# Two DMA transposes in place of PE transposes, and paired elementwise work, in the last job of a cross-network kernel

## The chip, the cores and the metric

The kernel runs on 1 core of one Trainium2 chip. The metric is the device time of one execution, in microseconds (us); smaller is better. PE is the TensorE matmul engine, PEld its weight load, ACT ScalarE, DVE VectorE, POOL GpSimd, and SP the engine whose queue issues most DMAs here ("SPq" in the profile; "ACTq" is ACT's queue). The profile's span is the time from the first to the last instruction on the core. It is about 1.8 us shorter than the measured time. A DMA is issued when a queue starts on it, and it has landed when all its bytes are there and those who wait for it may go on; from issue to landing it is called in flight.

## The reference

```python
B, F, D, L = 16384, 26, 16, 6          # Din = 26 * 16 = 416
x0: (16384, 416)   ws: (6, 416, 416)   bs: (6, 416)   # all bf16

def reference(x0, ws, bs):
    x = x0
    for l in range(6):
        proj = jnp.einsum('bd,de->be', x, ws[l]) + bs[l]
        x = x0 * proj + x
    return x
```

Each layer is a product with a 416 x 416 matrix, a bias, a multiplication by the input x0, and the addition of the residual x.

## The kernel before

The 16,384 rows are cut into 8 groups of 2,048 rows (0 to 7; `LAST` is 7), each of 4 chunks `j` of 512 rows. Features lie on the partitions: 416 is three tiles of 128 features (`NT = 3`) and a tail of 32. A job is one layer of one group; 48 jobs run in an order that lets the groups overlap. Except in the very last job, results are feature-major, so each finished group has to be turned to row-major by DMA transposes into the buffer `ost` before it can be stored:

```python
def output(g):
    s, s3 = xset[(g, L)], xtail[(g, L)]
    def turn(t):                                   # one feature tile, all 2,048 rows
        add("sp", lambda h: h.dma_start_transpose(
            ost[:, :, t * P:(t + 1) * P], xs[s][:, t * GC:(t + 1) * GC]),
            reads=[("x", s, t, j) for j in range(NJ)], writes=[("ost", t)], lane="ot", batch=g)
    turn(0)
    # ... the tail of 32 features: a DMA transpose into ot3 and a POOL copy into ost ...
    turn(1)
    turn(2)
    # ... one store of 2,048 x 416 values, 1.70 MB, from ost to out ...
```

`add` puts an instruction on an engine's queue and works out semaphore waits from the declared reads and writes. `turn(2)` of group 6 is called "the last output transpose" below, and the store after it "the store of group 6".

The last job (group 7, layer 5) is computed row-major, so that its result can be stored without a turn. It needs the residual row-major as well, and the kernel before turns it on PE (a product with the identity) for all three feature tiles, then copies it out of PSUM:

```python
def turn_main(kp, bks, ts):          # 128 x 128 PE transposes: 48 in all
    for j in range(NJ):
        for h2 in range(2):
            for t in ts:
                add("pe", ... h.transpose(psum_t(bks[j])[:, o:o + P], xcol(t, j, kk), ident[:, :]) ...)

def rows_out(kp, bks):               # PSUM -> x5n, 832 wide, 3 on ACT and 5 on DVE
    ...

def nat_mul(kk, j, b):               # evict on ACT, multiply by x0 on DVE, 416 wide
    add("act", lambda h: h.activation(o, bank(b, n=D), ACT_F.Copy), ...)
    add("dve", lambda h: h.tensor_tensor(o, o, x0v, ALU.mult), ...)
    # (the very last one multiplies straight out of PSUM, on DVE)

def nat_add(kk, j):                  # add the residual on DVE, 416 wide
    add("dve", lambda h: h.tensor_tensor(o, o, x5v, ALU.add), ...)

def nat_store(k0, k1, j0, j1, eng="sp"):
    dst = out[LAST * GC:B, :].rearrange("(j p k) f -> p j k f", j=NJ, k=KK)[:, j0:j1, k0:k1, :]
    add(eng, lambda h: h.dma_start(dst, on[:, j0:j1, k0:k1, :]), ...)
...
nat_store(0, 2, 0, NJ)               # after kk = 1: 832 KB, in runs of 2 rows = 1,664 bytes
...                                  # then 4 pieces after kk = 2 and during kk = 3, the last one from ACT's queue
```

In this order, (j p k), each partition holds 4 adjacent rows, and the four sub-blocks `kk` are strided columns of the chunk.

## Time and profile before

| kernel before | |
|---|---|
| median, 6 runs | 478.88 us (478.71 to 481.38) |
| span of the profiled run | 476.7 us |
| PE / DVE / ACT busy | 470.2 / 406.9 / 342.4 us |

From the page of the kernel before, the span, the busy times and the chain of waits (the dependences followed back from the last instruction, by engine):

```profile
span 476.7 us, 8467 instructions
...
PE 470.2 (99%) x3403; PEld 198.7 (42%) x3403; DVE 406.9 (85%) x714; ACT 342.4 (72%) x371; POOL 7.2 (2%) x14
...
PE 92%; SPq 4%; DVE 2%; ACT 1%; DMA 0%; issue 0%
```

PE bounds the kernel as a whole. The change touches only the end, so that end has to be read by itself. I call the first weight load of the last job its start. It is one line of the timeline of the kernel before (start in us, duration in us, then engine, line, operation, and destination <- source):

```profile
457.67 1.11 PEld L770 LDWEIGHTS ps<-ident,x 128*128 128x128 bf16 x16
```

The last pieces of the chain in the kernel before (start, duration, what; "..." stands for lines left out, some of them steps of 0.01 to 0.02 us called issue):

```profile
470.15 0.67 PE ps L800 x3
...
470.84 0.52 ACT x L828
...
471.37 0.53 ACT x L828
...
471.92 0.38 DVE x L830
...
473.56 0.51 DVE x L825
...
474.09 0.38 DVE x L835
```

At the end the chain goes from PE to ACT to DVE; the last addition ends at 474.47.

The DMA engines have their own story. Here are the last output transpose and the store of group 6 in SP's timeline of the kernel before (start, time to issue):

```profile
459.11 1.43 SPq L636 DMA_TRANSPOSE ost<-x  x1
464.19 0.38 SPq L655 DMA_DIRECT2D out_dram<-ost  x1
```

And this is what the DMA engines did afterwards, in stretches of the kernel before (the stretch and its length, the busy time of PE, PEld, DVE, ACT and POOL with their instruction counts, then PE's clock, the busy share of the 16 DMA engines, and GB/s; a share a little above 1 means overlapping packets):

```profile
465.50:468.50 3.00, 3.00 (x24) 1.57 (x22) 2.98 (x10) 2.51 (x6) 0.00 (x0) 1.00 1.05 351
468.50:470.00 1.50, 1.50 (x15) 0.65 (x13) 1.50 (x6) 1.47 (x4) 0.00 (x0) 1.00 1.10 335
470.00:472.50 2.50, 2.38 (x16) 1.28 (x12) 2.25 (x9) 1.77 (x4) 0.00 (x0) 1.00 1.06 376
473.00:474.00 1.00, 0.00 (x0) 0.00 (x0) 0.97 (x3) 0.00 (x0) 0.00 (x0) 1.00 0.24 83
474.00:475.50 1.50, 0.00 (x0) 0.00 (x0) 0.43 (x2) 0.00 (x0) 0.00 (x0) 1.00 0.92 321
```

The stores of groups 6 and 7 together are 3.41 MB, and they keep the DMA engines full from 465.2 to 473.0. Only then is there a hole, because the last pieces are not computed yet. So the kernel before is bound by compute at its end, with less than 1 us of spare DMA time.

### The profile page before, as it was taken

The page shows a single profiled execution, that of the slowest core. Times are in us where ns is not written, and L with a number is a line of the kernel's source. Part 1 is how long each engine was busy: PE and PEld are TensorE (multiplying, and loading weights), DVE is VectorE, ACT ScalarE, POOL GpSimd, SP SyncE. Part 2 cuts the span into 40 slices and gives each one's busy share as a digit, 9 for nine tenths or more (in the row PEclk, how much of TensorE's full clock was granted, in tenths as well). Part 3 has the DMA queues.
Part 4 walks back from the last instruction along what each step waited for, and adds up shares of the span by engine and source line. Part 5 has one row for each costly group of instructions (what it writes and reads, how often), then busy time and mean ns, then how long its engine had stood idle before and what let it go on. Part 6 is the DMA issues. An engine that isn't in the chain of part 4 may idle for free.

```text
span 476.7 us, 8467 instructions
## 1 busy us (share of the span) xinstructions
PE 470.2 (99%) x3403; PEld 198.7 (42%) x3403; DVE 406.9 (85%) x714; ACT 342.4 (72%) x371; POOL 7.2 (2%) x14
## 2 busy tenths in 40 slices
PE   8999999999999999999999999999999999999996
PEld 6344444444444444444444444434444444444353
DVE  2888888888888888898888879888888888888897
ACT  4677777777777777777777777777777777777775
POOL 0000000000000000000000000000000000000000
PEclk9999999999999999999999999999999999999999
DMA  8886920720102477379219932970000138026388
GB/s 232 179 176 144 195 66 1 157 65 1 34 1 46 76 212 156 75 168 242 57 35 211 207 80 40 189 236 0 2 15 21 26 64 231 0 45 159 108 145 286
DMA packets 131851, 52.27 MB, mean 110 GB/s; under 512 B 108122, under 2 KB 130404, under 8 KB 131812
## 3 DMA queue, kind: packets, MB, share of 16 engines
q1 hardware_dynamic: 131064, 51.20, 46.8%
q8 instruction: 26, 0.43, 0.4%
q10 hardware_dynamic: 748, 0.54, 0.3%
q14 instruction: 13, 0.11, 0.1%
HBM read 5.97 MB, written 13.63 MB: 41 GB/s over the span
## 4 chain that ended last, share of the span: by engine, by line
PE 92%; SPq 4%; DVE 2%; ACT 1%; DMA 0%; issue 0%
PE ps L456 75%; PE ps L477 7%; PE ps L497 7%; SPq L292 2%; PE ps L800 1%; PE ps L471 1%; DVE x L408 1%; DVE tw L403 1%; SPq L297 1%; PE ps L488 1%; SPq L285 0%; SPq L521 0%; ACT tw L394 0%; PE ps L770 0%; DMA x<-ost 0%; SPq L304 0%
## 5 line engine op out<-in xcount | busy, mean ns | idle before, releaser
L394 ACT ACTIVATE tw<-ps,bias 128x1024 bf16<-128x1024 f32 (+1 forms) x295 | 299.8, 1071 | 120.0 <-PE ps L477 75.9
L456 PE MATMUL ps<-x,wm 128*128 128x512 bf16 x1692 | 379.4, 379 | 0.0
L456 PEld LDWEIGHTS ps<-x,wm 128*128 128x128 bf16 x1692 | 159.0, 98 | 213.2 <-issue 28.3
L403 DVE TENSOR_TENSOR tw<-tw,x 128x1024 bf16<-128x1024 bf16 (+1 forms) x285 | 192.7, 685 | 53.9 <-ACT tw L394 53.6
L408 DVE TENSOR_TENSOR x<-tw,x 128x1024 bf16<-128x1024 bf16 (+1 forms) x285 | 182.5, 681 | 0.0
L477 PE MATMUL ps<-x,w 32*128 32x512 bf16 x512 | 39.2, 379 | 0.2 <-DMA x<-ost 0.2
L497 PE MATMUL ps<-x,wm 128*32 128x512 bf16 x564 | 33.0, 380 | 0.0
L434 ACT ACTIVATE ts<-ps,bias 128x512 bf16<-128x512 f32 x47 | 28.8, 701 | 0.0
L438 DVE TENSOR_TENSOR x<-ts,x 128x512 bf16<-128x512 bf16 x47 | 18.6, 417 | 3.0 <-DMA x<-x 3.0
L497 PEld LDWEIGHTS ps<-x,wm 128*32 128x32 bf16 x564 | 13.8, 96 | 17.6 <-issue 5.3
L477 PEld LDWEIGHTS ps<-x,w 32*128 32x128 bf16 x512 | 7.8, 92 | 27.9 <-issue 27.1
L436 DVE TENSOR_TENSOR ts<-ts,x 128x512 bf16<-128x512 bf16 x47 | 18.6, 418 | 0.0
L643 POOL COPY ost<-ot 128x512 bf16<-128x512 bf16 x7 | 6.3, 900 | 449.9 <-DMA ot<-x 449.9
L800 PE MATMUL ps<-wm,x 128*128 128x416 bf16 x48 | 9.4, 341 | 0.0
L568 DVE COPY x<-ps 128x512 bf16<-128x512 bf16 x4 | 1.7, 425 | 8.0 <-PE ps L561 8.0
L828 ACT ACTIVATE x<-ps 128x416 bf16<-128x416 f32 x15 | 7.1, 525 | 1.3 <-PE ps L800 1.1
L565 ACT ACTIVATE x<-ps 128x512 bf16<-128x512 bf16 x8 | 4.3, 594 | 4.8 <-PE ps L561 4.8
L800 PEld LDWEIGHTS ps<-wm,x 128*128 128x128 bf16 x48 | 5.1, 115 | 3.8 <-issue 1.4
L488 PE MATMUL ps<-x,w 32*32 32x512 bf16 x188 | 5.9, 374 | 0.0
L830 DVE TENSOR_TENSOR x<-x,x 128x416 bf16<-128x416 bf16 x15 | 5.4, 368 | 0.3 <-ACT x L828 0.2
L471 PE MATMUL ps<-x,w 32*32 32x512 bf16 x208 | 5.6, 385 | 0.0
L835 DVE TENSOR_TENSOR x<-x,x 128x416 bf16<-128x416 bf16 x16 | 5.6, 369 | 0.1
(35 smaller groups left out, 43.2 us busy)
## 6 DMA issues: line engine op xcount, KB each, us to landing
out_dram<-ost SPq DMA_DIRECT2D x7, 1664.0 KB, 6.8
x<-in_x_dram SPq DMA_DIRECT2D x7, 416.0 KB, 7.1
x<-x SPq DMA_DIRECT2D x24, 96.0 KB, 2.2
wm<-in_ws_dram SPq DMA_DIRECT2D x5, 312.0 KB, 3.4
x<-x SPq DMA_DIRECT2D x22, 64.0 KB, 2.0
x<-ost SPq DMA_DIRECT2D x28, 32.0 KB, 2.3
out_dram<-x SPq DMA_DIRECT2D x1, 832.0 KB, 4.3
x<-x SPq DMA_DIRECT2D x24, 32.0 KB, 1.9
```

The lines of the kernel that those rows point to most:

```text
L394: add("act", lambda h, a=a, w=w, b0=b0: h.activation(tw[r][:, a * CH:(a + w) * CH], psum[:, b0 * CH:(b0 + w) * CH], ACT_F.Identity, bias=b ...
L403: add("dve", lambda h, a=a, e=e: h.tensor_tensor(tw[r][:, a * CH:e * CH], tw[r][:, a * CH:e * CH], x0s[s0][:, i * GC + a * CH:i * GC + e * ...
L408: add("dve", lambda h, a=a, e=e: h.tensor_tensor(xs[so][:, i * GC + a * CH:i * GC + e * CH], tw[r][:, a * CH:e * CH], src(i, a, e), ALU.ad ...
L434: add("act", lambda h: h.activation(ts[r][:, :], bank(b), ACT_F.Identity, bias=bias[:, 3, l:l + 1], scale=1.0), reads=[("ps", b), "bias"], ...
L436: add("dve", lambda h: h.tensor_tensor(ts[r][:, :], ts[r][:, :], x03, ALU.mult), reads=[("ts", r)] + tok0, writes=[("ts", r)], release=True)
L438: add("dve", lambda h: h.tensor_tensor(x3s[so][:, :], ts[r][:, :], res, ALU.add), reads=[("ts", r)] + rtok, writes=[("x3", so), ("x3", so, ...
L456: add("pe", lambda h, t=t, j=j: h.matmul(bank(banks[j]), wm[l][:, t, ecols], src(t, j, j + 1), start=(first and t == 0), stop=(not first a ...
L471: add("pe", lambda h, q=q, j=j, r=r, c=c, o=o: h.matmul(psum[o, banks[j] * CH:(banks[j] + 1) * CH], w3[l][q, i * P + c * T32:i * P + (c + ...
L477: add("pe", lambda h, q=q, j=j, r=r: h.matmul(bank(banks[j]), w3[l][q, ecols], src[q, :], start=first, stop=not first, tile_position=(r * ...
L488: add("pe", lambda h, l=l, b=b, s3=s3, ri=ri, qi=qi, ro=ro, qo=qo: h.matmul(psum[qo, b * CH:(b + 1) * CH], w3[l][qi, NT * P:D], s3[qi, :], ...
L497: add("pe", lambda h, t=t, j=j, src=src, l=l, b=b, ro=ro, qo=qo: h.matmul(psum[qo, b * CH:(b + 1) * CH], wm[l][:, t, NT * P:D], src(t, j, ...
L800: add("pe", lambda h, t=t: h.matmul(bank(b, n=D), xcol(t, j, kk), wm[l][:, t, :], start=(first and t == 0), stop=(not first and t == NT - 1)),
```

## The change

The intent: take work off PE, DVE and ACT in the last job, where DVE is nearly always busy. Two of the three feature tiles of the residual are turned by DMA transposes, in a stretch in which the DMA queue is idle; only the third tile and the tail stay on PE. The multiplications and additions go in pairs of 832 columns. The bias rows become products over 32 rows, of which 31 are zero. The DMA transposes deliver rows in the order (j k p), so loads and stores of the last group take that order too, with runs of one row (832 bytes).

```diff
@@ load_last
-            add("sp", lambda h, j=j: h.dma_start(x0n7[:, j, :, :], perm(rows7, j)), ...
+            add("sp", lambda h, j=j: h.dma_start(
+                x0n7[:, j, :, :], rows7[j * CH:(j + 1) * CH, :].rearrange("(k p) f -> p k f", k=KK)), ...
@@ new
+    def rest_turn(t):
+        s = xset[(LAST, L - 1)]
+        if t == 0:
+            add("pool", lambda h: h.memset(warm[:, :], 0.0), writes=x0_all(s5) + x03_toks(s5) + ["x5 free"])
+        add("sp", lambda h: h.dma_start_transpose(
+            x5f[:, :, t * P:(t + 1) * P], xs[s][:, t * GC:(t + 1) * GC]),
+            reads=[("x", s, t, j) for j in range(NJ)] + ["x5 free"],
+            writes=[("x5n", j, t) for j in range(NJ)], lane=f"x5_{t}", batch=0)
@@ after the first job
+    add("pool", lambda h: h.memset(brow[:, :], 0.0), writes=["brow"])
@@ tile loop
+        if (g, l) == (LAST, L - 2) and i < NT - 1:
+            rest_turn(i)
@@ last job (cut)
-        return src(t, j, j + 1).rearrange("p (m k) -> p m k", k=KK)[:, :, kk]
+        return src(t, j, j + 1)[:, kk * P:(kk + 1) * P]
-    def turn_main ... rows_out            # 48 PE transposes, 8 copies 832 wide
+    def turn_last(j, b)                   # 16 PE transposes (third tile only)
+    def turned_out(j, b)                  # 2 copies 1,024 wide, on ACT
+    def turn_tails(bks)                   # tails, 1 copy 512 wide, on ACT
-                        bank(bks[j], n=D), ones[r * T32:r * T32 + 1, :], brow[r * T32:r * T32 + 1, :],
+                bank(bks[j], n=D), ones[q, :], brow[q, :], start=False, stop=False, tile_position=(r * T32, 0)),
+    def nat_mul(kk, j, n=2):              # pairs of chunks
+    def nat_add(kk, j, n=2):
-        dst = out[LAST * GC:B, :].rearrange("(j p k) f -> p j k f", j=NJ, k=KK)[:, j0:j1, k0:k1, :]
+        dst = out[LAST * GC:B, :].rearrange("(j k p) f -> p j k f", j=NJ, k=KK)[:, j0:j1, kk, :]
-    nat_store(0, 2, 0, NJ) ; (2, 4, 0, 2) ; (3, 4, 2, 3) ; (2, 3, 2, NJ) ; (3, 4, 3, NJ, "act")
+    nat_store(0, 0, NJ) ; (1, 0, NJ) ; (2, 0, NJ) ; (3, 0, 3) ; (3, 3, 4, "act")
```

More of the change, by code (lines that the diff above doesn't have):

```diff
@@ L625, in load_last @@
         for j in range(NJ):
-            add("sp", lambda h, j=j: h.dma_start(x0n7[:, j, :, :], perm(rows7, j)),
+            add("sp", lambda h, j=j: h.dma_start(
+                x0n7[:, j, :, :], rows7[j * CH:(j + 1) * CH, :].rearrange("(k p) f -> p k f", k=KK)),
                 writes=(x0_all(sn) + x03_toks(sn) if j == 0 else []) + [("n7", j)], lane="n7", batch=0)
@@ L629, in load_last @@
             add("sp", lambda h, j=j: h.dma_start(brow[j * T32:j * T32 + 1, :], bs[L - 1:L, :]),
-                writes=[("brow", j)] + (["brow"] if j == 0 else []), lane="brow", batch=0)
+                reads=["brow"], writes=[("brow", j)], lane="brow", batch=0)
     def output(g):
@@ L650, in output @@
         o = ost[:, :, :].rearrange("p (j k) f -> p j k f", j=NJ)
-        parts = [("(j k p) f -> p j k f", 0, NJ)]
-        if g == 0:
-            parts = [("(j p k) f -> p j k f", 0, NJ)]
-        for pat, j0, j1 in parts:
-            add("sp", lambda h, pat=pat, j0=j0, j1=j1: h.dma_start(
-                rows[j0 * CH:j1 * CH, :].rearrange(pat, j=j1 - j0, k=KK), o[:, j0:j1, :, :]),
-                reads=[("ost", t) for t in range(NT + 1)],
-                writes=[("out", g, j0)], lane="out", batch=g)
+        pat = "(j p k) f -> p j k f" if g == 0 else "(j k p) f -> p j k f"
+        add("sp", lambda h: h.dma_start(rows.rearrange(pat, j=NJ, k=KK), o),
+            reads=[("ost", t) for t in range(NT + 1)], writes=[("out", g)], lane="out", batch=g)
         free_x.append(s)
         free_3.append(s3)
+    x5f = x0s[s5][:, 0:XW + CH].rearrange("p (a f) -> p a f", f=D)
+    def rest_turn(t):
[6 more added lines that the diff above has]
+            writes=[("x5n", j, t) for j in range(NJ)], lane=f"x5_{t}", batch=0)
     items = []
@@ L757, in xcol @@
     def xcol(t, j, kk):
-        return src(t, j, j + 1).rearrange("p (m k) -> p m k", k=KK)[:, :, kk]
+        return src(t, j, j + 1)[:, kk * P:(kk + 1) * P]
     def x3col(j, kk):
-        return s3[quad(g, l, j)[1], :].rearrange("p (m k) -> p m k", k=KK)[:, :, kk]
-    first_use = {"x5": True, "on": True}
-    def turn_main(kp, bks, ts):
-        for j in range(NJ):
-            for h2 in range(2):
-                for t in ts:
-                    o = h2 * CH + t * P
-                    add("pe", lambda h, j=j, t=t, kk=2 * kp + h2, o=o: h.transpose(
-                        psum_t(bks[j])[:, o:o + P], xcol(t, j, kk), ident[:, :]),
-                        reads=[stok(t, j), "ident"], writes=[("ps", bks[j])])
-    def turn_tails(kp, bks):
-        for h2 in range(2):
-            for j in range(NJ):
-                r, q = quad(g, l, j)
-                o = h2 * CH + NT * P
-                add("pe", lambda h, j=j, q=q, r=r, kk=2 * kp + h2, o=o: h.matmul(
-                    psum_t(bks[j])[:, o:o + T32], x3col(j, kk), ident[q, q], is_transpose=True,
-                    tile_position=(r * T32, 0)),
-                    reads=tok3 + ["ident"], writes=[("ps", bks[j])])
-    def rows_out(kp, bks):
-        for j in range(NJ):
-            extra = x0_all(s5) + x03_toks(s5) if first_use.pop("x5", None) else []
-            eng = "act" if j == 0 or (kp and j == 2) else "dve"
-            dst = x5n[:, j, 2 * kp:2 * kp + 2, :]
-            sp_ = psum_t(bks[j]).rearrange("p (a f) -> p a f", a=2)[:, :, 0:D]
-            if eng == "act":
-                add("act", lambda h, dst=dst, sp_=sp_: h.activation(dst, sp_, ACT_F.Copy),
-                    reads=[("ps", bks[j])], writes=extra + [("x5n", j, kp)])
-            else:
-                add("dve", lambda h, dst=dst, sp_=sp_: h.tensor_copy(dst, sp_),
-                    reads=[("ps", bks[j])], writes=extra + [("x5n", j, kp)])
+        return s3[quad(g, l, j)[1], kk * P:(kk + 1) * P]
+    first_use = {"on": True}
     def nat_full(kk, j, b, first, ts=range(NT)):
@@ L803, in nat_full, with turn_last @@
                 reads=[stok(t, j), ("wm", l)], writes=[("ps", b)])
-    def nat_rows(kk, bks, first):
-        for part in range(2):
+    def turn_last(j, b):
+        t = NT - 1
+        for a in (j, j + 1):
+            for kk in range(KK):
+                o = ((a - j) * KK + kk) * P
+                add("pe", lambda h, a=a, kk=kk, o=o: h.transpose(
+                    psum_t(b)[:, o:o + P], xcol(t, a, kk), ident[:, :]),
+                    reads=[stok(t, a), "ident"], writes=[("ps", b)])
@@ L807, in nat_rows, with turned_out, turn_tails @@
+    def turned_out(j, b):
+        t = NT - 1
+        add("act", lambda h: h.activation(
+            x5n[:, j:j + 2, :, t * P:NT * P].rearrange("p j k f -> p (j k) f"),
+            psum_t(b).rearrange("p (a f) -> p a f", f=P), ACT_F.Copy),
+            reads=[("ps", b), "x5 free"], writes=[("x5n", j, t), ("x5n", j + 1, t)])
+    def turn_tails(bks):
+        for kk in range(KK):
             for j in range(NJ):
                 r, q = quad(g, l, j)
-                st, sp_ = first and part == 0, not first and part == 1
@@ L810, in nat_rows @@
-                if part == 0:
-                    add("pe", lambda h, j=j, q=q, r=r, st=st: h.matmul(
-                        bank(bks[j], n=D), x3col(j, kk), w3[l][q, :], start=st, stop=False,
-                        tile_position=(r * T32, 0)),
-                        reads=tok3 + [("w3", l, r)], writes=[("ps", bks[j])])
-                else:
-                    add("pe", lambda h, j=j, r=r, sp_=sp_: h.matmul(
-                        bank(bks[j], n=D), ones[r * T32:r * T32 + 1, :], brow[r * T32:r * T32 + 1, :],
-                        start=False, stop=sp_, tile_position=(r * T32, 0)),
-                        reads=["ones", ("brow", r)], writes=[("ps", bks[j])])
@@ L821, in nat_mul @@
-    def nat_mul(kk, j, b):
-        extra = x0_all(so) + x03_toks(so) if first_use.pop("on", None) else []
-        o, x0v = on[:, j, kk, :], x0n7[:, j, kk, :]
-        if kk == KK - 1 and j == NJ - 1:
-            add("dve", lambda h: h.tensor_tensor(o, bank(b, n=D), x0v, ALU.mult),
-                reads=[("ps", b), ("n7", j)], writes=extra + [("on", j, kk)])
-        else:
-            add("act", lambda h: h.activation(o, bank(b, n=D), ACT_F.Copy),
-                reads=[("ps", b)], writes=extra + [("on", j, kk)])
-            add("dve", lambda h: h.tensor_tensor(o, o, x0v, ALU.mult),
-                reads=[("on", j, kk), ("n7", j)], writes=[("on", j, kk)])
@@ L833, in nat_add @@
-    def nat_add(kk, j):
-        o, x5v = on[:, j, kk, :], x5n[:, j, kk, :]
+                add("pe", lambda h, b=bks[j], j=j, kk=kk, q=q, r=r: h.matmul(
+                    psum_t(b)[:, kk * T32:(kk + 1) * T32], x3col(j, kk), ident[q, q], is_transpose=True,
+                    tile_position=(r * T32, 0)),
+                    reads=tok3 + ["ident"], writes=[("ps", bks[j])])
+        b = bks[0]
+        assert bks == list(range(b, b + NJ))
+        sp_ = psum[:, b * CH:(b + NJ) * CH].bitcast(BF16).rearrange("p (j c) -> p j c", j=NJ)[:, :, 0:KK * T32]
@@ new lines, in turn_tails, with nat_rows @@
+        add("act", lambda h: h.activation(
+            x5n[:, :, :, NT * P:D], sp_.rearrange("p j (k f) -> p j k f", k=KK), ACT_F.Copy),
+            reads=[("ps", b) for b in bks] + ["x5 free"], writes=[("x5n", j, NT) for j in range(NJ)])
+    def nat_rows(kk, bks, first=True):
+        for j in range(NJ):
+            r, q = quad(g, l, j)
+            add("pe", lambda h, j=j, q=q, r=r: h.matmul(
+                bank(bks[j], n=D), x3col(j, kk), w3[l][q, :], start=first, stop=False, tile_position=(r * T32, 0)),
+                reads=tok3 + [("w3", l, r)], writes=[("ps", bks[j])])
+        for j in range(NJ):
+            r, q = quad(g, l, j)
+            add("pe", lambda h, j=j, q=q, r=r: h.matmul(
+                bank(bks[j], n=D), ones[q, :], brow[q, :], start=False, stop=False, tile_position=(r * T32, 0)),
+                reads=["ones", ("brow", r)], writes=[("ps", bks[j])])
@@ new lines, in nat_out @@
+    def nat_out(kk, j, bks):
+        extra = x0_all(so) + x03_toks(so) if first_use.pop("on", None) else []
+        add("act", lambda h: h.activation(on[:, j, kk, :], bank(bks[j], n=D), ACT_F.Copy),
+            reads=[("ps", bks[j])], writes=extra + [("on", j, kk)])
+    def nat_mul(kk, j, n=2):
+        o, x0v = on[:, j:j + n, kk, :], x0n7[:, j:j + n, kk, :]
+        toks = [("on", a, kk) for a in range(j, j + n)]
+        add("dve", lambda h: h.tensor_tensor(o, o, x0v, ALU.mult),
+            reads=toks + [("n7", a) for a in range(j, j + n)], writes=toks)
@@ L835, in nat_add @@
+    def nat_add(kk, j, n=2):
+        o, x5v = on[:, j:j + n, kk, :], x5n[:, j:j + n, kk, :]
+        toks = [("on", a, kk) for a in range(j, j + n)]
         add("dve", lambda h: h.tensor_tensor(o, o, x5v, ALU.add),
-            reads=[("on", j, kk), ("x5n", j, kk // 2)], writes=[("on", j, kk)])
+            reads=toks + [("x5n", a, t) for a in range(j, j + n) for t in range(NT + 1)], writes=toks)
     stores = [0]
-    def nat_store(k0, k1, j0, j1, eng="sp"):
-        dst = out[LAST * GC:B, :].rearrange("(j p k) f -> p j k f", j=NJ, k=KK)[:, j0:j1, k0:k1, :]
-        add(eng, lambda h: h.dma_start(dst, on[:, j0:j1, k0:k1, :]),
-            reads=[("on", j, kk) for j in range(j0, j1) for kk in range(k0, k1)],
-            writes=[("out7", k0, j0)], lane=f"out7_{stores[0]}", batch=0)
-        stores[0] += 1
@@ L847, in bass_standalone__cross_network_dcn__recsys_kernel @@
-    bka, bkb = take(NJ), take(NJ)
-    last = KK - 1
-    def layer_full(kk, bks, ts=range(NT)):
-        for j in range(NJ):
-            nat_full(kk, j, bks[j], False, ts)
-            nat_mul(kk, j, bks[j])
-            if kk < last:
-                if j:
-                    nat_add(kk, j - 1)
-            elif j == 1:
-                nat_add(kk, 0)
-                nat_add(kk, 1)
-                nat_store(kk - 1, kk + 1, 0, 2)
-            elif j == 2:
-                nat_add(kk, 2)
-                nat_store(kk, kk + 1, 2, 3)
-        nat_add(kk, NJ - 1)
@@ L866, in bass_standalone__cross_network_dcn__recsys_kernel @@
-    turn_main(0, bka, (0, 1))
-    turn_tails(0, bka)
-    nat_rows(0, bkb, True)
-    for j in range(NJ):
-        nat_full(0, j, bkb[j], False, (0, 1))
-    turn_main(0, bka, (2,))
-    rows_out(0, bka)
-    layer_full(0, bkb, (2,))
-    turn_main(1, bka, (0, 1, 2))
-    turn_tails(1, bka)
-    rows_out(1, bka)
-    nat_rows(1, bkb, True)
-    layer_full(1, bkb)
-    nat_store(0, 2, 0, NJ)
-    nat_rows(2, bka, True)
-    layer_full(2, bka)
-    nat_store(2, 3, 2, NJ)
-    nat_rows(3, bkb, True)
@@ L884, in bass_standalone__cross_network_dcn__recsys_kernel, with nat_store @@
-    layer_full(3, bkb)
-    nat_store(3, 4, 3, NJ, "act")
+    def nat_store(kk, j0, j1, eng="sp"):
+        dst = out[LAST * GC:B, :].rearrange("(j k p) f -> p j k f", j=NJ, k=KK)[:, j0:j1, kk, :]
+        add(eng, lambda h: h.dma_start(dst, on[:, j0:j1, kk, :]),
+            reads=[("on", j, kk) for j in range(j0, j1)],
+            writes=[("out7", kk, j0)], lane=f"out7_{stores[0]}", batch=0)
+        stores[0] += 1
+    a0, a1, a2, a3 = bka = take(NJ)
+    b0, b1, b2, b3 = take(NJ)
+    bks = {0: bka, 1: [b0, b3, b1, a0], 2: [a1, a2, a3, b2], 3: [b0, b3, b1, a0]}
@@ new lines, in bass_standalone__cross_network_dcn__recsys_kernel @@
+    for j in range(NJ):
+        nat_full(0, j, bks[0][j], True, (0, 1))
+    turn_tails([b0, b1, b2, b3])
+    nat_rows(0, bks[0], False)
+    turn_last(0, b1)
+    turned_out(0, b1)
+    for j in range(NJ):
+        if j == 2:
+            turn_last(2, b2)
+        nat_full(0, j, bks[0][j], False, (2,))
+        nat_out(0, j, bks[0])
+    nat_mul(0, 0)
+    nat_add(0, 0)
+    nat_mul(0, 2)
+    nat_rows(1, bks[1])
+    for j in range(NJ):
+        nat_full(1, j, bks[1][j], False)
+        nat_out(1, j, bks[1])
+        if j == 1:
+            turned_out(2, b2)
+            nat_mul(1, 0)
+            nat_add(1, 0)
@@ new lines, in bass_standalone__cross_network_dcn__recsys_kernel @@
+    nat_add(0, 2)
+    nat_store(0, 0, NJ)
+    nat_mul(1, 2)
+    nat_add(1, 2)
+    nat_store(1, 0, NJ)
+    nat_rows(2, bks[2])
+    for j in range(NJ):
+        nat_full(2, j, bks[2][j], False)
+        nat_out(2, j, bks[2])
+        if j % 2:
+            nat_mul(2, j - 1)
+            nat_add(2, j - 1)
+    nat_store(2, 0, NJ)
+    kk = KK - 1
+    nat_rows(kk, bks[kk])
+    for j in range(NJ):
+        nat_full(kk, j, bks[kk][j], False)
+        nat_out(kk, j, bks[kk])
+        if j:
+            first, n = ((0, 2), (2, 1), (3, 1))[j - 1]
+            nat_mul(kk, first, n)
+            nat_add(kk, first, n)
+        if j == 2:
+            nat_store(kk, 0, 3)
@@ L887, in bass_standalone__cross_network_dcn__recsys_kernel @@
+    nat_store(kk, 3, 4, "act")
     pr.emit()
```

## The prediction

> **What bounds the kernel now.** The page gives PE 470.2 us busy of a span of 476.7 (99%), DVE 407, ACT 342, clock 1.0; the chain of waits is 92% PE. None of this is touched before the last job, the last layer of the last group of rows, computed row-major. In the timeline that tail runs from 457.7 to 476.7 us. At its end the chain leaves PE: last matmul at 472.4, then ACT and DVE to 474.5, then the last store. DVE is busy without a gap from 454.3 to 471.5 and almost so to 474.5.
>
> Half-microsecond windows show a second limit. The store of the group before (1.70 MB) starts moving at 465.2, and from there to 473.0 the DMA engines are saturated (share 1.01 to 1.11; 331 to 356 GB/s for that store, up to 393 for the 1,664-byte runs of the last group). Only 473.0 to 474.0 has a hole, about 0.8 us; writing ends near 475.8.
>
> **What the change removes, adds and moves.**
> - PE: 32 of 48 transposes go (24 took 1.34 us on the chain: 1.8 us). The 48 main products (0.187 us each, 9.0 us) stay. Bias rows as 32-row products: four take 0.18 us either way.
> - DVE: five 832-wide copies from PSUM go (2.6 us); 32 multiplications and additions of 0.30 us become 14 pairs of about 0.53 us (1,024 wide takes 0.64, 512 wide 0.33) and 4 singles. DVE work of the tail: 12.2 to about 8.6 us.
> - ACT: three copies (0.81 us) become two 1,024-wide (about 1.0) and one 512-wide (0.6); 16 evictions of 0.44 us for 15. About 0.6 us more; ACT becomes the fuller elementwise engine (about 9.6 us).
> - DMA: two transposes (2.2 us to issue, about 3 us of engines each) come at about 446 and 448, in the empty slot 445 to 452. The second overlaps the next group's first output transpose by perhaps 1 us, but that group's later transposes wait for DVE, so its store still issues near 464.2. The last store comes in 425 KB pieces of 832-byte runs, which move at about 348 GB/s and not 385.
>
> **On the critical path.** PE does 2.3 us of work, then still waits for the last tile of the layer before (DVE, 460.1 to 461.7). I expect short stalls of PE for banks that ACT has not emptied, about 1 us in all. Last matmul: 472.4 to about 471.0. Last DVE addition: 474.5 to about 472.3. So compute gains about 2 us. But the bytes do not shrink: 3.41 MB from 465.2 on, at 348 GB/s, needs until 475.0. Both issuing queues share the same 16 DMA engines (the Trainium skill, "Trainium Kernel Development and Optimization", Key Constraints), so issuing the last piece from ACT adds no bandwidth; in this trace the rate never exceeds 393 GB/s. The gain is what the hole cost: 0.8 us, not 2. Elsewhere nothing changes.
>
> **Prediction.** Median 478.3 us (before 479.15); 8 times in 10 between 477.2 and 479.3. Faster by over 2%: 0.01; within 2%: 0.98; slower by over 2%: 0.01.
>
> **What would show the steps.** Right: the transposes land before 455; the store of the group before issues at 464.2 +- 0.5; last addition at 472.3 +- 0.7; DMA share about 1 without a hole from 465.2 to 475.0; span 475.3 to 476.3. Wrong: a hole in DMA near the end (compute still binds); last addition after 473.5; that store later than 465.
>
> **What would make it wrong.** Stores faster than 348 GB/s: the gain nears 2 us. Transposes that delay that store: the end slips with it. More PE stalls on ACT: compute returns to 474 and the gain vanishes.

## The result, and the profile after

The kernel after took 479.38 us (median of 6 runs, 479.08 to 479.95), and 478.76 us when it was run again later. A ratio here is the mean time of one kernel's fast runs over that of the other's of the same rounds, so not quite the ratio of the medians. It was 1.0003 (95% interval 0.9982 to 1.0023) the first time and 1.0000 (0.9979 to 1.0020) the second. The change gained nothing that can be measured. The first median lies 0.08 us above the predicted range and the second inside it; that range holds the unchanged kernel (478.88) as well, so falling into it confirms nothing. The predicted gain of 0.8 us did not come.

The same lines of the page, kernel after:

```profile
span 477.8 us, 8395 instructions
...
PE 469.5 (98%) x3371; PEld 196.3 (41%) x3371; DVE 403.5 (84%) x695; ACT 342.9 (72%) x372; POOL 8.1 (2%) x16
...
PE 97%; ACT 2%; DVE 1%; issue 0%; POOL 0%; POOLq 0%
```

PE, DVE and total instructions fell as intended, and yet the profiled span is 1.1 us longer. Most of that is not the change. The last job starts 0.84 us later, and all of that arises in the first microseconds of the program. Compare PE's timeline, kernel before:

```profile
5.72 0.62 PE L541 MATMUL ps<-ident 128*128 128x128 bf16 x8
6.18 1.46 PE L456 MATMUL ps<-x,wm 128*128 128x512 bf16 x6
```

and kernel after:

```profile
5.74 1.03 PE L541 MATMUL ps<-ident 128*128 128x128 bf16 x8
6.56 2.13 PE L456 MATMUL ps<-x,wm 128*128 128x512 bf16 x6
```

The same products ran slower here. The Trainium skill, "TensorE: Matmul & The Clock Gate", Part 1, says that PE starts at half clock until it has been busy for a window, and that the window runs freely, so the number of slow products varies from run to run. The traces agree. Their first record of the clock, full from then on, stands at 5.47 us in the kernel before and at 7.92 us in the kernel after (it is in the packed trace; the stretches of the views show 1.00 before it too, because they count time without a record as full clock). In the kernel after the products that began at 6.56, 6.99 and 7.42 us took 634 ns each, the one at 7.84 took 423, and those from 8.10 on took 379; in the kernel before all six began after the record and took 379. A second reason shows up in other runs: in before_half, a variant of the kernel before below, the same products waited 2.46 us for the first weights:

```profile
8.59 2.72 PE L456 MATMUL ps<-x,wm 128*128 128x512 bf16 x6 [2.46 <-DMA wm<-in_ws_dram]
```

The clock of that trace stood at 0.50 from 8.5 to 11.8 us, after the wait. Over the 13 traces, the first 32-row product of the program begins anywhere from 13.2 to 17.3 us. That is more than everything the change does. **So from here on I count times from the start of the last job**, and that start is, in the kernel after:

```profile
458.51 1.37 PEld L778 LDWEIGHTS ps<-wm,x 128*128 128x128 bf16 x8
```

The last pieces of the chain, kernel after:

```profile
469.98 0.65 PE ps L778 x3
...
470.65 0.52 ACT x L829
...
471.18 0.53 ACT x L829
...
471.73 0.60 DVE x L835
...
473.64 0.30 DVE x L835
...
473.96 0.37 DVE x L841
```

The last addition ends at 474.33, that is 15.82 us after the start of the last job and not 16.80: compute did gain 0.98 us. The DMA lines tell where it went. SP's timeline, kernel after:

```profile
459.95 3.34 SPq L637 DMA_TRANSPOSE ost<-x  x1
465.38 0.39 SPq L653 DMA_DIRECT2D out_dram<-ost  x1
```

The last output transpose took 3.34 us to issue and not 1.43, and the store of group 6 issued 6.87 us after the start of the last job and not 6.52. The DMA engines afterwards, kernel after:

```profile
466.50:469.50 3.00, 2.81 (x24) 1.25 (x25) 2.70 (x5) 2.55 (x6) 0.00 (x0) 1.00 1.06 347
469.50:472.50 3.00, 2.70 (x21) 1.16 (x20) 2.56 (x6) 2.38 (x6) 0.00 (x0) 1.00 1.09 339
472.50:476.00 3.50, 0.00 (x0) 0.00 (x0) 1.76 (x5) 0.25 (x1) 0.00 (x0) 0.94 1.11 331
476.00:476.50 0.50, 0.00 (x0) 0.00 (x0) 0.00 (x0) 0.00 (x0) 0.00 (x0) 0.50 0.98 283
476.50:477.00 0.50, 0.00 (x0) 0.00 (x0) 0.00 (x0) 0.00 (x0) 0.00 (x0) 0.50 0.04 10
```

There is no hole any more: the DMA engines are full from 466.4 to 476.4, at a rate that sinks from 347 to 331 GB/s, and then a thin rest runs until about 476.8. The last piece, issued at 474.37, queued behind the others and landed 3.0 us after its issue, where the kernel before's took 1.7 us.

### The profile page after: what moved, and what is told of

It reads as the page before. It is cut to its first block, busy times and chain, and to the rows that moved or that the text cites. A ratio compares the mean times of both kernels' runs of the same rounds, so it can differ in the third digit from the quotient of the medians.

```text
span 477.8 us, 8395 instructions
## 1 busy us (share of the span) xinstructions
PE 469.5 (98%) x3371; PEld 196.3 (41%) x3371; DVE 403.5 (84%) x695; ACT 342.9 (72%) x372; POOL 8.1 (2%) x16
## 4 chain that ended last, share of the span: by engine, by line
PE 97%; ACT 2%; DVE 1%; issue 0%; POOL 0%; POOLq 0%
PE ps L456 78%; PE ps L477 7%; PE ps L497 7%; PE ps L471 1%; PE ps L778 1%; PE ps L561 1%; ACT x L829 1%; PE ps L488 1%; PE ps L541 1%; ACT x L795 0%; DVE x L841 0%; DVE x L835 0%; ACT x L565 0%; PE ps L789 0%; PE ps L818 0%
## 5 line engine op out<-in xcount | busy, mean ns | idle before, releaser
L835 DVE TENSOR_TENSOR x<-x,x 128x832 bf16<-128x832 bf16 (+1 forms) x9 | 4.9, 540 | 2.1 <-ACT x L829 2.1
L561 PE MATMUL ps<-ident,x 128*128 128x128 bf16 x64 | 5.3, 242 | 0.3 <-ACT x L565 0.3
```

## The experiments

Theory D: in the kernel after, the end is set by the DMA engines, by when the store of group 6 starts and how fast 3.41 MB drain; what compute gained is lost in their queue. Theory C, the rival: the chain of PE, ACT and DVE still sets the end, and the change simply gains little. All 13 traces in one table, in us after the start of the last job (the profile gives the span to 0.1 us, so the ends are good to 0.05):

| kernel | store of group 6 issued | last DVE addition ends | span ends | median, and before in the same rounds |
|---|---|---|---|---|
| before | 6.52 | 16.80 | 19.03 | 478.88 |
| after | 6.87 | 15.82 | 19.29 | 479.38, 478.88 |
| after_again | 6.67 | 15.80 | 19.15 | 478.76, 479.18 |
| after_half (wrong) | 6.74 | 15.88 | 18.35 | 478.46, 479.02 |
| before_half (wrong) | 6.53 | 16.81 | 19.02 | 479.63, 479.02 |
| no_turn (wrong) | 6.51 | 15.85 | 19.03 | 479.39, 479.02 |
| long_runs (wrong) | 6.50 | 15.78 | 18.72 | 478.96, 479.02 |
| dve_turned | 6.91 | 15.07 | 19.44 | 479.75, 479.18 |
| split | 5.84 | 15.82 | 18.31 | 478.49, 479.18 |
| split_again | 5.91 | 15.80 | 18.36 | 478.16, 479.08 |
| split_dve | 5.89 | 15.03 | 18.34 | 478.36, 479.18 |
| one_turn (wrong) | 6.92 | 15.83 | 19.37 | 478.60, 478.31 (one run each) |
| three_turns | 7.81 | 15.83 | 20.26 | 480.21, 478.31 (one run each) |

"Wrong" marks kernels that give a wrong result.

### after_half and before_half: half the bytes of group 6

```diff
 # after_half
-        add("sp", lambda h: h.dma_start(rows.rearrange(pat, j=NJ, k=KK), o),
+        n = 2 if g == LAST - 1 else NJ
+        add("sp", lambda h: h.dma_start(rows.rearrange(pat, j=NJ, k=KK)[:, 0:n], o[:, 0:n]),
 # before_half
+        if g == LAST - 1:
+            parts = [("(j k p) f -> p j k f", 0, 2)]
```

> The kernel after, with only half of the rows of group 6 (the group before the last) stored; the other half of that output is left unwritten on purpose. Times are counted from the first weight load of the last job, so that the start of the run drops out. Theory D (the end is bound by the DMA engines, which the stores of the last two groups keep full): with 0.85 MB less to move the last bytes no longer queue, the span ends about 2.2 us after the last DVE addition, so the last job takes about 18.0 us and not 19.3; the run is 1 to 1.3 us faster than the kernel after. Theory C (the chain of PE, ACT and DVE still ends the kernel after): the last job keeps 19.3 us, the time does not move.

> The kernel before with the same half store of group 6 (wrong on purpose). In the kernel before the stores had an empty microsecond before the last piece, so D expects no gain: last job 19.0 us as before, within 0.2. If the kernel before was bound by the DMA engines too, it gains over 0.5 us. The difference of the two half-store kernels is what the change gains when the DMA engines are out of the way: D expects about 1.0 us, the difference of their last additions (16.8 and 15.8 us after the start of the last job).

Measured: the spans of after_half (last job from 457.45) and before_half (from 461.48) are

```profile
span 475.8 us, 8395 instructions
```

```profile
span 480.5 us, 8467 instructions
```

With half the bytes the kernel after ended at 18.35, 0.80 to 0.94 us sooner than its two full traces (1.0 to 1.3 was expected), while its last addition had not moved (15.88). The kernel before ended at 19.02 and gained nothing. So D holds on both sides: the kernel after is bound by the DMA engines at its end and the kernel before is not. With the DMA engines out of the way the change is worth 19.02 - 18.35 = 0.67 us. D had expected 1.0; the span still ended 2.47 us after the last addition, where in before_half it ended 2.21 after it. The 312 KB piece issued 0.7 us before the last one was still in flight, which may be why; no run tests it. The medians point the same way but are blurred by the start (before_half began its last job at 461.48 us): ratio 0.9979 (0.9958 to 1.0001) for after_half and 1.0015 (0.9986 to 1.0044) for before_half.

### no_turn: without the two DMA transposes

```diff
-        add("sp", lambda h: h.dma_start_transpose(
-            x5f[:, :, t * P:(t + 1) * P], xs[s][:, t * GC:(t + 1) * GC]), ...)
```

> The kernel after without the two DMA transposes of the residual (the residual of columns 0 to 255 is stale, wrong on purpose). If they are what delays the store of group 6, its issue goes back from 6.9 to 6.5 us after the start of the last job and the end comes 0.3 to 0.4 us sooner. If they are harmless, issue stays at 6.9 us and the time does not move.

Measured: SP's timeline of no_turn has

```profile
460.03 1.32 SPq L637 DMA_TRANSPOSE ost<-x  x1
465.08 0.38 SPq L653 DMA_DIRECT2D out_dram<-ost  x1
```

The last output transpose is quick to issue again (1.32 us), the store issues at 6.51 us as in the kernel before, and the span ends at 19.03, 0.12 to 0.26 us sooner than in the two traces of the kernel after (0.3 to 0.4 was expected). So the DMA transposes can delay the store of group 6, although they themselves had landed more than 11 us before it issued. The delay is much smaller than the longer issue suggests: the store waits for the last output transpose to land, and from issue to landing that took 5.1 us in the kernel before, 5.0 in no_turn, 5.4 in the kernel after and 5.2 in after_again. An issue longer by 1.7 to 2 us thus cost 0.4 us or less. Taking the delay away is not enough to gain: with compute done 0.95 us sooner than in the kernel before (15.85), no_turn ends when the kernel before does, as far as the spans tell. The rest of the loss is in the draining of the bytes.

### long_runs: the old pattern of the last stores

```diff
-        dst = out[LAST * GC:B, :].rearrange("(j k p) f -> p j k f", j=NJ, k=KK)[:, j0:j1, kk, :]
+        dst = out[LAST * GC:B, :].rearrange("(j p k) f -> p j k f", j=NJ, k=KK)[:, j0:j1, k0:k1, :]
-    nat_store(0, 0, NJ) ... (1, 0, NJ) ... (2, 0, NJ) ... (kk, 0, 3) ... (kk, 3, 4, "act")
+    nat_store(0, 2, 0, NJ) ... (2, 4, 0, 2) ... (2, 4, 2, 3) ... (2, 4, 3, 4, "act")
```

> The kernel after with the stores of the last group in the pattern of the kernel before (1,664-byte runs, rows permuted, wrong on purpose), same bytes. If the shorter runs cost bandwidth, the last group moves at about 380 GB/s and not 333, and the writing of 3.4 MB ends about 0.5 us sooner, unless the first store of the last group, now later, leaves a hole. If run length does not matter, the rate stays near 335 GB/s.

Measured, in stretches of long_runs (the first is still mostly group 6, in 832-byte runs; in the second the first store of the last group, in 1,664-byte runs, is alone in flight; in the third two or three pieces of the last group are):

```profile
469.00:471.50 2.50, 2.50 (x21) 1.11 (x19) 2.18 (x5) 1.89 (x5) 0.00 (x0) 1.00 1.10 341
472.20:473.20 1.00, 0.23 (x2) 0.00 (x0) 0.97 (x3) 0.77 (x2) 0.00 (x0) 1.00 1.07 394
474.60:475.80 1.20, 0.00 (x0) 0.00 (x0) 0.00 (x0) 0.00 (x0) 0.00 (x0) 1.00 1.00 349
```

The kernel after moved the last group at 331 GB/s, but nearly always with several stores in flight. In after_half one of its 832-byte stores ran alone for a while, and faster:

```profile
471.50:472.50 1.00, 0.00 (x0) 0.00 (x0) 0.97 (x3) 0.24 (x1) 0.00 (x0) 1.00 1.06 354
```

Like compared with like, the longer runs moved at 394 and not 354 GB/s alone, and at 349 and not 331 with several in flight. So run length counts, but by 5 to 11% and not by the 14% (333 to 380) that was expected; that the number of stores in flight counts too is what these stretches suggest (and in the kernel before the fall from 351 to 335 GB/s, around the issue of the second store), but no run varies it alone. The span ended at 18.72, 0.43 to 0.57 us sooner than the kernel after, in spite of a hole of about 0.7 us in the writing. Not all of that is the longer runs: the store of group 6 issued at 6.50 here, 0.17 to 0.37 us sooner than in the kernel after. Counted from that issue, the end came after 12.22 us and not 12.42 to 12.48, so 0.2 to 0.3 us are left. Both DMA transposes are in this kernel, and their delay varies (6.50 to 6.91 over the five full or halved kernels with both); with the last output transpose taking 3.01 us to issue, the store here was not late at all.

### after_again: the spread of one kernel

> The kernel after once more, unchanged, for the spread of one kernel. In six traces so far the first products of the program came at 13.3 to 17.3 us, in kernels that are the same up to there, and the last job took 19.3 us in the kernel after and 19.0 in the kernel before. If the start is chance, it will be anywhere in 13 to 17 us here while the last job takes 19.0 to 19.4 us. If the new clearing of the bias rows on POOL delays the start, the start is at 14.3 us or more again. The issue of the last output transpose of group 6 is expected to take about 3 us again and not 1.4, and the store of group 6 to issue 6.5 to 6.9 us after the start of the last job.

Measured: the first 32-row product of the kernel after unchanged began at 13.19 us this time (14.36 the first time), and it ended its last job after 19.15 us. The start is chance and not the new POOL clearing, and the last job repeats within 0.14 us. The last output transpose took 3.16 us to issue and the store of group 6 issued at 6.67, as expected.

### dve_turned: faster compute alone

```diff
-        add("act", lambda h: h.activation(            # turned_out: PSUM -> x5n, 1,024 wide
-            ..., psum_t(b).rearrange("p (a f) -> p a f", f=P), ACT_F.Copy),
+        add("dve", lambda h: h.tensor_copy(
+            ..., psum_t(b).rearrange("p (a f) -> p a f", f=P)),
```

> The kernel after with the two 1,024-wide copies of the PE transposes moved from ACT to DVE. If ACT is what holds the chain of the last job (its evictions queue behind those copies), the last addition comes 0.5 to 1.0 us sooner than 15.8 us after the start of the last job. Theory D (DMA engines bind the end) expects the span of the last job to stay at 19.0 to 19.4 us all the same. Theory C (compute binds) expects it to shrink by what the last addition gains.

Measured: the last addition of dve_turned, in DVE's timeline, ended at 472.53, or 15.07 us after the start of the last job at 457.46:

```profile
471.76 0.37 DVE L835 TENSOR_TENSOR x<-x,x 128x416 bf16<-128x416 bf16 x1
472.16 0.37 DVE L841 TENSOR_TENSOR x<-x,x 128x416 bf16<-128x416 bf16 x1
```

Compute was 0.73 to 0.75 us faster than in the kernel after, so the copies on ACT did hold the chain. And the span ended at 19.44, not sooner at all; the time did not move either (1.0006, 0.9991 to 1.0022). Theory C falls here: compute got faster and the end did not.

### split, split_again and split_dve: start the stores sooner

```diff
-        turn(2)
-        add("sp", lambda h: h.dma_start(rows.rearrange(pat, j=NJ, k=KK), o), ...)
+        for c in range(2):           # group 6 only
+            add("sp", lambda h, c=c: h.dma_start_transpose(
+                ost[:, 2 * KK * c:2 * KK * (c + 1), t * P:(t + 1) * P],
+                xs[s][:, t * GC + 2 * CH * c:t * GC + 2 * CH * (c + 1)]), ...)
+        for c in range(2):
+            add("sp", lambda h, c=c: h.dma_start(
+                rows.rearrange(pat, j=NJ, k=KK)[:, 2 * c:2 * c + 2], o[:, 2 * c:2 * c + 2]), ...)
```

split_dve is this and the edit of dve_turned together; split_again is split once more.

> The kernel after with the last output transpose of group 6 and its store cut in two halves, so that the first half of the store can issue while the second half is still being turned; compute of the last job unchanged, result correct. Theory D: the stores start about 0.8 us sooner and the last job ends sooner by nearly that, at 18.3 to 18.7 us, with the last addition still at 15.8. Theory C: no change.

> Both edits, split and dve_turned; result correct. Theory D: with the DMA engines started sooner the earlier last addition can count too: last job at 17.7 to 18.4 us, about 1 us under the kernel before (0.2% of the time). If it is no faster than split, compute is not what is left.

> The split kernel once more, unchanged, as the version that is correct and ended soonest: the last job in 18.2 to 18.5 us again (kernel before 19.0, kernel after 19.2 to 19.3), the stores of group 6 issuing at 5.8 to 6.7 us, and a median 0.5 to 1 us under that of the kernel before in the same rounds, with an interval that may still touch 1 because the start of the program varies by more than that.

Measured, SP's timeline and the span of split (last job from 458.49):

```profile
464.33 1.12 SPq L665 DMA_DIRECT2D out_dram<-ost  x2
```

```profile
span 476.8 us, 8344 instructions
```

It issued its first store at 5.84, about 0.9 us sooner than the kernel after, left compute where it was (15.82), and ended at 18.31; its repeat at 18.36. The end moved by what the start of the stores moved, as D expected and C did not. In the stretches of split there is a small hole again,

```profile
472.50:474.00 1.50, 0.00 (x0) 0.00 (x0) 1.43 (x5) 0.23 (x1) 0.00 (x0) 1.00 1.11 333
474.00:474.50 0.50, 0.00 (x0) 0.00 (x0) 0.31 (x1) 0.00 (x0) 0.00 (x0) 0.77 0.18 48
474.50:476.00 1.50, 0.00 (x0) 0.00 (x0) 0.00 (x0) 0.00 (x0) 0.00 (x0) 0.50 0.82 284
```

so here the last piece of compute and the draining of the bytes come out together. split_dve shows it from the other side: with compute 0.79 us sooner (15.03) it ends at 18.34, no sooner than split, and it has no such hole near the end (472.5 to 475.0: share 1.11). My expectation of up to 0.6 us beyond split for split_dve was wrong: DMA binds there again at the same time.

split is correct and beats the kernel before by about 0.2%: ratio 0.9981 (0.9965 to 0.9997), and again 0.9974 (0.9953 to 0.9996). split_dve was 0.9991 (0.9968 to 1.0015), with one run of 481.57 among its six.

### one_turn and three_turns: why the last output transpose is slow to issue

```diff
 # one_turn
+        if t == 1:
+            return
 # three_turns
+        if t == 0:
+            add("sp", lambda h: h.dma_start_transpose(
+                x5f[:, :, 2 * P:3 * P], xs[s][:, 0:GC]), ..., lane="x5_extra", batch=0)
```

> The kernel after with one of the two DMA transposes of the residual (the second left out, wrong on purpose). In three kernels with both, the last output transpose of group 6 took 3.0 to 3.4 us to issue; in three with none, 1.3 to 1.4. Theory P (the queue stretches some transposes by about 1 us, by their place in the sequence of transposes): the stretch falls on another one, and the last takes under 2.2 us. Theory L (each transpose shortly before adds its share of delay): the last takes about 2.2 to 2.5 us. In both the store of group 6 issues at 6.5 to 6.7 us after the start of the last job.

> The kernel after with a third DMA transpose of 128 columns into a part of the residual that is overwritten later (result correct). Theory P: the stretch moves to another transpose and the last output transpose of group 6 takes under 2.2 us to issue, although there is more work in the queue. Theory L: it takes 3.2 us or more, and the store of group 6 issues at 6.9 us or later after the start of the last job.

Measured, SP's timeline of one_turn:

```profile
458.87 3.44 SPq L637 DMA_TRANSPOSE ost<-x  x1
464.35 0.38 SPq L653 DMA_DIRECT2D out_dram<-ost  x1
```

and of three_turns:

```profile
459.97 3.85 SPq L637 DMA_TRANSPOSE ost<-x  x1
465.95 0.38 SPq L653 DMA_DIRECT2D out_dram<-ost  x1
```

Both theories miss. One added transpose already stretches the last issue to 3.44 us, as much as two do (3.0 to 3.4); P wanted under 2.2, L wanted 2.2 to 2.5. Three give 3.85, which only L allows; but there the third transpose also pushed the group's own ones back (the first began 3.67 us before the start of the last job, where it was 5.93 in the kernel after), so the store's delay is not that of the issue alone. My expectation that the store of one_turn would issue at 6.5 to 6.7 was wrong too (6.92). Why an earlier DMA transpose lengthens the issue of a later one stays open.

These two runs are useful for something else. three_turns shifts the store of group 6 by 0.94 us against the kernel after (7.81 and 6.87) with the last addition where it was (15.83), and the span ends 0.97 us later. In every unsplit kernel with the new stores and all bytes, the end comes a fixed time after that issue: 12.42, 12.48, 12.52, 12.45, 12.45 and 12.53 us (after, after_again, no_turn, one_turn, three_turns, dve_turned; span end minus store issue in the table), whatever compute does. The equal time alone would prove little: the kernel before has 12.51 as well, and 12.49 with half the bytes, so there it is chance. Split, its repeat and split_dve have 12.45 to 12.47 from their first store. The proof is that here the end follows the bytes and the issue and not the last addition.

## Why the prediction was right or wrong

- **That DMA, not compute, would cap the gain: right.** The prediction said that 3.41 MB do not shrink and that the hole would close. It closed, and half the bytes, an earlier start, a later start and a faster compute each did what that requires. The Trainium skill's sentence on the shared 16 engines ("Trainium Kernel Development and Optimization", Key Constraints) agrees: the last piece, issued from ACT's queue, landed after 3.0 us and not 1.7.
- **The gain of 0.8 us: wrong, there was none.** Counted from the start of the last job, the predicted middle (475.8 us) is an end at 18.1, and the profiled run ended at 19.29. The step that failed is "3.41 MB from 465.2 on, at 348 GB/s, needs until 475.0", with the end 0.8 us after that. Its terms: the stores began moving at 466.4 - 458.51 = 7.9 us and not at 7.5 (+0.35, the later issue); the full-rate part took 10.0 us and not 9.8 (+0.2, as the rate sank to 331; the kernel before shows the same fall, from 351 to 335 GB/s, around 468.96, where the next store is issued, so 348 was too high for a queue of stores); a thin rest of about 20 KB ran on for 0.35 us; and the end came 1.05 us after the last byte where I had allowed 0.8 (+0.25). Together about 1.15 us, which is the miss.
- **"So its store still issues near 464.2": wrong by 0.15 to 0.35 us** in the two traces of the kernel after. I had looked at the engines' idle slot and at the first overlap, and not at how long the later output transposes take to land. no_turn points to the added transposes as the cause; but long_runs, with both, issued its store at 6.50 all the same, and the mechanism is open. The prediction's own signs of an error, a store after 465 and a last addition after 473.5, both came (465.38 and 474.33); with the 0.84 us of the later start taken off they are 464.54 and 473.49, just short of it.
- **Compute gains 2 us: half wrong.** The last matmul gained 1.0 us and the last addition 0.98, against 1.4 and 2.2 predicted. The chain of the kernel after runs through ACT, whose 1,024-wide copies (1.02 us each) hold up evictions and banks; moving them to DVE gained 0.75 us. That ACT would become the fuller engine was predicted; its cost was set too low (10.4 us for its three groups in the last job, against about 9.6). It did not matter for the time.
- **The other costs: right where it was checked.** The 128-wide PE transposes of the last job fell from 3.6 us of busy PE to 1.5 (1.8 less predicted), the pairs took 0.59 us each (0.5 to 0.6 in sequence, 0.53 predicted), the 1,024-wide copies 1.02 us (1.0 predicted), and both added DMA transposes landed by 453.7 us (before 455 predicted).
- **Within 2%: right**, at 1.0003 and 1.0000. The comparison of medians alone could not have told more: the start of the program varies by up to 4 us from run to run.

## What to carry to other kernels

When compute at the end of a kernel is shortened, ask what the stores behind it need: if bytes over measured rate already reach to the end, look for an earlier start, fewer bytes or longer runs; here each of these moved the end and faster compute did not. Work moved to an idle DMA slot can be paid for again, as here by shorter runs and by transfers that land later. A transfer rate read off with one store in flight need not hold for a queue of them. And when effects are well under 1% of the time, count them inside the trace from a fixed event, because the start of the program can vary by more than the effect.

## What the Trainium skill lacked or had wrong

- "DMA: Bandwidth & Descriptors", Specifications, gives 512 bytes or more as the transfer size for line rate. Here stores to HBM in 832-byte runs moved at 354 GB/s with one store in flight and at 331 with several, and in 1,664-byte runs at 394 and 349, so that row alone does not tell what longer runs still gain.
- The same page, "DMA Transpose (X-bar)", does not say that the time to issue a DMA transpose depends on the ones before it: the same transpose took 1.3 to 1.4 us as it was, 3.0 to 3.4 with one or two transposes added 11 to 13 us earlier, and 3.85 with three added. Its landing moved by at most 0.4 us with one or two added.
- No page that I read tells of a thin rest at the end of a long backlog: after 10 us at full rate the kernel after had about 0.3 us at 8 to 25 GB/s.
